# First gate and value products of a chunked-attention SwiGLU kernel, made in halves of 256 tokens

## The chip, the core and the metric

The kernel runs on one core of a Trainium2 chip. The metric is the time of one execution on the device in microseconds (us); lower is better. TensorE (PE in the rows) multiplies, VectorE (DVE), ScalarE (ACT) and GpSimd (POOL) work on tiles, SyncE (SP) issues most of the DMA transfers. Each engine runs its instructions in the order of its own queue; between the engines semaphores say when a tile is ready.

## What is computed

```python
# attention in chunks of 64 tokens: B=8, H=8, S=576, D=64
scores = (1 / sqrt(D)) * q_c @ k_c.T            # one chunk with itself
attn = exp(scores - max); attn = attn / (sum(attn) + 1e-9)
out = attn @ v_c                                # -> x: 4608 tokens x 512
# gated layer: d_model 512, d_ff 1536
rms = sqrt(mean(x * x) + 1e-6); xn = x / rms * rms_g
g = xn @ w_gate; silu = g / (1 + exp(-g))
y = (silu * (xn @ w_val)) @ w_out               # 4608 x 512
```

## The kernel before

The 4608 tokens go in tiles of 512 (`TT`), each of two units of 256 (`UT`). The first three tiles are worked in plain form, the others in pairs. Every product of the gated layer is made three times, as high part by high part, high by low and low by high (`up`, L591; `down`, L626): a single precision number is split in two parts that TensorE multiplies fully. d_ff is cut into 12 blocks `f` of 128. For one `f` of a plain tile, `up` makes 12 products 128x512 into the bank `ps_g` (4 slices of d_model, 3 products each) and 12 into `ps_v`; `gated` then makes the silu on ScalarE (L609, with a load of its function table where another function ran before), multiplies it with `ps_v` on VectorE (L613), and splits the result into `gh` (L614, ScalarE) and `gl` (L618, VectorE); `down` of the `f` before follows on TensorE.

Both banks come from `ps_h`, a pool of two banks. The `ps_g` of the next `f` therefore lies in the bank that the silu of this `f` reads, and its first product waits for that silu. The two other pools are `ps_a` (two banks) and `ps_acc` (four, for the sums of `down` from the first `f` on).

Ahead of the first products stands a prologue. Units 0 and 1 (four half units 0 to 3) go through scores (`scores`, L265), softmax (`softmax` L278 to L282 for unit 0, `softmax_both` L570 to L576 for unit 1), a transpose of the exponentials (`att_transpose` L323 on TensorE, copied by L324 on ScalarE), the row sums (`softmax_sum` L287 to L289), the value products (`att_values` L450), the scaling by the sums (`first_norm` L536), the squares (`first_squares` L548 on ScalarE), the root of their mean (`first_root`, L144 on ScalarE and L145 on GpSimd) and the scaling by it (`first_scale` L556 and L560, ScalarE). Then the tokens of a unit are turned: `x_turn_unit` transposes them on TensorE (L510, four blocks 128x128 to a bank), `x_high_unit` makes the high part `xh` (L516, ScalarE) and `x_low_unit` the low part `xl` (L522, VectorE).

Beside this the weights are converted from 64-bit raw words, block after block: `conv_load` (L169, a DMA of SyncE), `conv_start` (L177 and L178, each 128x1024, ScalarE), `conv_join` (L186, L187, L190 on VectorE, L203 on ScalarE for the high part, L205 as a DMA of SyncE that puts a copy `wfd` into DRAM), `conv_end` (L211, VectorE, the low part). `conv_step` loads block n+4, starts n+1, joins n and ends n-1. In the program text the prologue ends with `conv_start(0)` and `conv_step(EARLY)`, that is three steps; later steps stand inside `gated`. In the first tile, at `f` = 0, `load_unit` (L233 to L235) issues the transfers `qt`, `kt`, `vt` of unit 2, and its scores follow on TensorE.

In this part of the program a scheduler sets each engine's order: it takes what is ready by its estimate, by a priority that follows the place in the program text. `urgent()` raises the priority of the silu and what follows it by `URGENT` = 300. Only from the second tile on is TensorE's order written by hand.

Of the kernel before, what the change touches and what calls it, by code (L numbers as in the profile page):

```python
# [13 lines left out]
AF = mybir.ActivationFunctionType  # L14
# [9 lines left out]
UT = 256  # L24
NU = N // UT
TT = 512
# [3 lines left out]
NDT = DM // P  # L30
DFF = 1536
NF = DFF // P
SCALE = D**-0.5
# [46 lines left out]
def tile_chunk_attn_swiglu(  # L80
# [124 lines left out]
                nc.sync.dma_start(wfd[f], w)  # L205

    def conv_end(n):
        if 0 <= n < len(pairs):
            w, parts = conv.pop(n)
            hi, lo = (parts[:, i].rearrange("p i c -> p (i c)") for i in range(2))  # L210
            nc.vector.tensor_tensor(lo, w, hi.bitcast(F32), op=ALU.subtract)  # L211
# [350 lines left out]
    def softmax_both(u, banks):  # L562
        both = [state[2 * u + s] for s in range(2)]
        es = [att.tile([P, NPAIR, 2, CH], F32, name="e") for _ in both]
        mx = small.tile([P, 2, 2, NPAIR, 1], F32, name="mx_u")
        for st, e in zip(both, es):
            st["e"] = e
        for j in range(2):
            by_row = banks[j].rearrange("p s (a k) -> p s a k", k=CH)
            nc.vector.tensor_reduce(mx[:, j], by_row, axis=AX.X, op=ALU.max)  # L570
            for s, (st, e) in enumerate(zip(both, es)):
                nc.vector.tensor_tensor(
                    e[:, :, j], st["s"][j], mx[:, j, s].broadcast_to([P, NPAIR, CH]), op=ALU.subtract
                )
        for e in es:
            nc.scalar.activation(e, e, AF.Exp, scale=SCALE)  # L576

    def softmax_whole(u, banks):
        softmax_both(u, banks)
# [3 lines left out]
        nc.vector.tensor_scalar_add(rs, rs, 1e-9)  # L583
        nc.vector.reciprocal(rs, rs)

    def up(wh, wl, f, name):
        ps = bank(ps_h, name)
        for dt in range(NDT):
            cols = slice(dt * P, (dt + 1) * P)
            for i, (a, b) in enumerate(((wh, xh), (wh, xl), (wl, xh))):  # L590
                nc.tensor.matmul(  # L591
                    ps,
                    a[f][:, cols],
                    b[dt],
                    start=(dt == 0 and i == 0),
                    stop=(dt == NDT - 1 and i == 2),
                )
        return ps

    def gated(f, at, then):  # L600
        pg = up(wgh, wgl, f, "ps_g")
        pv = up(wvh, wvl, f, "ps_v")
        if 0 in at:
            then()
        sg = tmp_tile("sg")
        gh = gp.tile([P, TT], F32R, name="gh")
        gl = gp.tile([P, TT], F32R, name="gl")
        with urgent():
            nc.scalar.activation(sg, pg, AF.Silu)  # L609
        if 1 in at:  # L610
            then()
        with urgent():
            nc.vector.tensor_tensor(sg, pv, sg, op=ALU.mult)  # L613
            nc.scalar.copy(gh, sg)  # L614
        if 2 in at:
            then()
        with urgent():
            nc.vector.tensor_tensor(gl, sg, gh.bitcast(F32), op=ALU.subtract)  # L618
        return gh, gl
# [505 lines left out]
    first_squares(0)  # L1125
    first_root(0)
    first_scale(0, False)
    att_transpose(2)
    softmax_sum(2)
    att_transpose(3)  # L1130
    softmax_sum(3)
    o = two_banks(ps_h, "ps_o")
    att_values(2, o)
    first_norm(2)
    o = two_banks(ps_acc, "ps_o")
# [3 lines left out]
    first_root(1)  # L1139
    first_scale(1, False)  # L1140
    for d in range(0, NDT, 2):
        x_turn_unit(0, d, ps_a)
        x_high_unit(0, d)
        x_low_unit(0, d)
    for d in range(0, NDT, 2):
        x_turn_unit(1, d, ps_a)
        x_high_unit(1, d)
        x_low_unit(1, d)
    conv_start(0)
    conv_step(EARLY)  # L1150

    for t in range(PLAIN):
        if t == 1:
# [36 lines left out]
        acc = [ps_acc.tile([P, DM], F32, tag="acc", name=f"acc{s}") for s in range(NSUB)]  # L1190
        prev = None
        for f in range(NF):
            g = gated(f, CONVS[f % 2], conv_step)
            if t == 0:
                if f in (0, 5):
                    u = 2 + (f == 5)
                    load_unit(u)
                    sc = two_banks(ps_a, "ps_s")
                    for i in (2 * u, 2 * u + 1):
                        scores(i, sc)  # L1200
                    if f:
                        softmax_rows(u, sc)
                    else:
                        softmax_whole(u, sc)
                elif f in (2, 7):
                    for i in (2 * u, 2 * u + 1):
                        att_transpose(i)
                elif f in (3, 8):
                    o = two_banks(ps_a, "ps_o")
                    for i in (2 * u, 2 * u + 1):  # L1210
                        att_values(i, o)
                    norm_unit(u, o)
                if f == NF - 1:
                    x_transpose((0, 1))
            elif t == 1 and f == NF - 1:
                for dt in range(NDT):
                    x_split(dt, blocks(x)[:, :, dt], slice(0, TT))
            if t == 1:
                if f % 2 == 0:
                    save_plain(f // 2)  # L1220
                for todo in made.pop(0):
                    todo()
            if t:
                half()
            if prev is not None:
                down(acc, f - 1, *prev)
            if t:
                half()
            prev = g
# [89 lines left out]
```

## Time and profile before

| | us |
|---|---|
| runs | 901.83, 903.35, 903.49 (median 903.35) |
| the profiled execution | 903.58 |
| its span in the trace | 901.8 |
| TensorE busy in the span | 879.7 (98%) |
| VectorE, ScalarE, GpSimd busy | 604.8, 456.2, 183.9 |

The profiled execution lasts 1.8 us longer than its span; this lies around the first and the last instruction. The first 40 us, with the prologue, are the only longer part of the span in which TensorE is not busy throughout. The place to read is therefore one moment: when the second `ps_g`, that of `f` = 1, begins, and what set it.

### The profile page before, as it was taken

The numbers are of one execution on the slowest core, as the hardware profiler recorded it, in microseconds if no ns is written. First come the engines' busy times: TensorE is split into PE (matmuls) and PEld (weight loads), VectorE is DVE, ScalarE is ACT, GpSimd is POOL, SyncE is SP. The second block draws the span as 40 slices with busy tenths as digits, with TensorE's granted clock in tenths as the row PEclk, the third lists the DMA queues.
The fourth block names the chain that finished last, engine by engine and source line by source line (L and its number), as shares of the span: only waits on it lengthen the run. The fifth ranks groups of instructions, "written<-read, shape, count | busy, mean of one in ns | idle before, by whom it ended". The sixth has DMA issues, their size and how long they took to land.

```text
span 901.8 us, 17425 instructions
## 1 busy us (share of the span) xinstructions
PE 879.7 (98%) x6828; PEld 722.8 (80%) x6828; DVE 604.8 (67%) x962; ACT 456.2 (51%) x775; POOL 183.9 (20%) x157
## 2 busy tenths in 40 slices
PE   4899999999999999999999999999999999999998
PEld 3688888888888888888878888888888888888886
DVE  6999865464568755885577997555769953334775
ACT  5998934343445564544545644336447522222452
POOL 0004040243200000233323002333330004323200
PEclk9799999999999999999999999999999999999999
DMA  9699999777977864887797877685866794445442
GB/s 353 258 346 330 334 331 352 244 253 236 302 250 237 259 207 155 308 275 261 260 324 281 306 282 262 247 295 189 310 233 244 287 360 164 155 156 201 180 164 94
DMA packets 85794, 231.84 MB, mean 257 GB/s; under 512 B 8912, under 2 KB 45264, under 8 KB 71504
## 3 DMA queue, kind: packets, MB, share of 16 engines
q1 hardware_dynamic: 84656, 230.20, 72.4%
q8 instruction: 54, 0.88, 0.4%
q10 hardware_dynamic: 1056, 0.52, 0.2%
q14 instruction: 28, 0.23, 0.1%
HBM read 167.25 MB, written 63.44 MB: 256 GB/s over the span
## 4 chain that ended last, share of the span: by engine, by line
PE 90%; DMA 4%; DVE 2%; ACT 1%; POOL 1%; issue 1%; SPq 0%; POOLq 0%; ACTq 0%; DVEq 0%
PE ps_g L591 11%; PE acc L626 11%; PE ps_v L591 11%; PE ps_c L819 10%; PE ps_b L819 10%; PE ps_a L819 9%; PE ps_b L1032 5%; PE ps_c L1032 5%; PE ps_a L1032 5%; PE ps_d L819 5%; DMA wr<-wsd 3%; PE ps_d L1032 3%; PE ps_o L392 2%; PE ps_s L265 2%; DMA x<-qT_dram 1%
## 5 line engine op out<-in xcount | busy, mean ns | idle before, releaser
L819 PE MATMUL ps_c<-xp,wr 128*128 128x512 f32 x432 | 104.6, 391 | 0.5 <-DMA wr<-wsd 0.5
L819 PE MATMUL ps_b<-xp,wr 128*128 128x512 f32 x432 | 104.4, 391 | 0.0
L819 PE MATMUL ps_a<-xp,wr 128*128 128x512 f32 x432 | 103.6, 390 | 0.0
L591 PE MATMUL ps_g<-xh,parts 128*128 128x512 f32 x288 | 97.0, 397 | 0.6 <-ACT xh L516 0.6
L591 PE MATMUL ps_v<-xh,parts 128*128 128x512 f32 x288 | 95.2, 391 | 0.0
L819 PEld LDWEIGHTS ps_c<-xp,wr 128*128 128x128 f32 x432 | 80.6, 188 | 17.6 <-issue 0.7
L819 PEld LDWEIGHTS ps_a<-xp,wr 128*128 128x128 f32 x432 | 80.9, 188 | 16.9
L819 PEld LDWEIGHTS ps_b<-xp,wr 128*128 128x128 f32 x432 | 80.7, 188 | 17.0
L626 PE MATMUL acc<-parts,gh 128*128 128x512 f32 x288 | 89.9, 393 | 0.0
L907 POOL TENSOR_TENSOR g<-u,u 128x512 f32<-128x512 f32 x18 | 23.2, 1290 | 268.3 <-ACT u L875 130.3
L591 PEld LDWEIGHTS ps_g<-xh,parts 128*128 128x128 f32 x288 | 54.7, 190 | 12.7 <-ACT xh L516 1.0
L591 PEld LDWEIGHTS ps_v<-xh,parts 128*128 128x128 f32 x288 | 54.5, 189 | 11.3
L939 ACT CAST gh<-g 128x512 fp32r<-128x512 f32 x72 | 43.5, 621 | 37.3 <-PE ps_b L1032 13.3
L626 PEld LDWEIGHTS acc<-parts,gh 128*128 128x128 f32 x288 | 53.2, 188 | 11.2
L944 DVE TENSOR_TENSOR gl<-g,gh 128x512 fp32r<-128x512 f32 x72 | 50.3, 705 | 15.8 <-PE ps_a L1032 7.0
L897 POOL TENSOR_TENSOR p<-p,p 128x512 f32<-128x512 f32 x36 | 46.8, 1311 | 52.9 <-DVE rs L353 35.8
L591 PE MATMUL ps_g<-xl,parts 128*128 128x512 f32 x144 | 56.7, 394 | 0.0
L591 PE MATMUL ps_v<-xl,parts 128*128 128x512 f32 x144 | 56.3, 391 | 0.0
L626 PE MATMUL acc<-parts,gl 128*128 128x512 f32 x144 | 56.2, 390 | 0.0
L875 ACT ACTIVATE p<-p 128x512 f32<-128x512 f32 x36 | 22.8, 633 | 58.4 <-POOL p L897 52.6
L819 PE MATMUL ps_d<-xp,wr 128*128 128x512 f32 x216 | 52.3, 391 | 0.0
L884 DVE TENSOR_TENSOR u<-ps_b,p 128x512 f32<-128x512 f32 x36 | 24.5, 687 | 40.0 <-PE ps_b L819 36.4
(150 smaller groups left out, 1705.2 us busy)
## 6 DMA issues: line engine op xcount, KB each, us to landing
wr<-wsd SPq DMA_DIRECT2D x63, 1024.0 KB, 7.1
wo<-osd SPq DMA_DIRECT2D x30, 1024.0 KB, 7.7
raw<-w_up_dram SPq DMA_DIRECT2D x12, 1024.0 KB, 9.9
vt<-v_dram SPq DMA_DIRECT2D x18, 512.0 KB, 6.0
wsd<-parts SPq DMA_DIRECT2D x18, 512.0 KB, 8.2
qt<-qT_dram SPq DMA_DIRECT2D x17, 512.0 KB, 5.2
kt<-kT_dram SPq DMA_DIRECT2D x17, 512.0 KB, 6.1
away_e<-e SPq DMA_DIRECT2D x28, 256.0 KB, 3.3
```

The source lines that it names most:

```text
L265: nc.tensor.matmul(st["s"][j][c * CH : (c + 1) * CH, pr], st["q"][rows, pr, tok : tok + CH], st["k"][rows, pr, tok : tok + CH], start=True ...
L392: nc.tensor.matmul(st["o"][(2 * c + t) * Q : (2 * c + t + 1) * Q, h * D : (h + 1) * D], eT[c][rows, t, h], vt[rows, c, h], start=True, sto ...
L591: nc.tensor.matmul(ps, a[f][:, cols], b[dt], start=(dt == 0 and i == 0), stop=(dt == NDT - 1 and i == 2),)
L626: nc.tensor.matmul(acc[s], a[:, cols], b, start=(f == 0 and i == 0), stop=(f == NF - 1 and i == 2),)
L819: nc.tensor.matmul(ps, w[:, a, m, cols], xp[:, b, kt], start=start and kt == 0 and i == 0, stop=stop and kt == 1 and i == 2, skip_group_ch ...
L875: nc.scalar.activation(t, t if src is None else src, AF.Silu)
L884: nc.vector.tensor_tensor(kp["u2"], b["b"], kp["p1"], op=add)
L897: nc.gpsimd.tensor_tensor(kp["p5"], kp["p1"], kp["p5"], op=add)
L907: nc.gpsimd.tensor_tensor(g[:, 0, 1], kp["u2"], kept[0]["u2"], op=mult)
L939: nc.scalar.copy(gh, src)
L944: nc.vector.tensor_tensor(gl, src, pair[0].bitcast(F32), op=ALU.subtract)
L1032: nc.tensor.matmul(banks[m][name], w[:, (0, 1, 0)[k], m * P : (m + 1) * P], (gh, gh, gl)[k], start=opens and i == 0 and k == 0, stop=not ( ...
```

## The change

The first block, `f` = 0 of the first tile, is made in two halves of 256 tokens. `up` gets its bank and a slice of tokens; `gated` gets `begun`, the two banks that already hold the first half's products, and makes the second half's into them. Where 24 products 128x512 stood, there are now 48 of 128x256. Unit 0 is turned and split right behind the row sums of unit 1 in the program text, in banks of `ps_acc`, and block 0 of the weights is started and joined before the transposes of unit 1 and ended behind the split of unit 0. The exps of `softmax_both` get a priority raised by 600. `ps_o` of half unit 2 comes from `ps_acc` instead of `ps_h`, since `begun` now holds `ps_h`. Behind `begun` stand `conv_load(4)`, `conv_start(1)` and two conversion steps from block 1 on, in place of the three from block 0.

```diff
--- before.py
+++ after.py
@@ -205,7 +205,7 @@
                 nc.sync.dma_start(wfd[f], w)
 
     def conv_end(n):
-        if 0 <= n < len(pairs):
+        if n in conv:
             w, parts = conv.pop(n)
             hi, lo = (parts[:, i].rearrange("p i c -> p (i c)") for i in range(2))
             nc.vector.tensor_tensor(lo, w, hi.bitcast(F32), op=ALU.subtract)
@@ -572,8 +572,9 @@
                 nc.vector.tensor_tensor(
                     e[:, :, j], st["s"][j], mx[:, j, s].broadcast_to([P, NPAIR, CH]), op=ALU.subtract
                 )
-        for e in es:
-            nc.scalar.activation(e, e, AF.Exp, scale=SCALE)
+        with tc.high_priority(offset=2 * URGENT):
+            for e in es:
+                nc.scalar.activation(e, e, AF.Exp, scale=SCALE)
 
     def softmax_whole(u, banks):
         softmax_both(u, banks)
@@ -583,23 +584,27 @@
         nc.vector.tensor_scalar_add(rs, rs, 1e-9)
         nc.vector.reciprocal(rs, rs)
 
-    def up(wh, wl, f, name):
-        ps = bank(ps_h, name)
+    def up(wh, wl, f, ps, tokens=slice(0, TT)):
         for dt in range(NDT):
             cols = slice(dt * P, (dt + 1) * P)
             for i, (a, b) in enumerate(((wh, xh), (wh, xl), (wl, xh))):
                 nc.tensor.matmul(
-                    ps,
+                    ps[:, tokens],
                     a[f][:, cols],
-                    b[dt],
+                    b[dt][:, tokens],
                     start=(dt == 0 and i == 0),
                     stop=(dt == NDT - 1 and i == 2),
                 )
         return ps
 
-    def gated(f, at, then):
-        pg = up(wgh, wgl, f, "ps_g")
-        pv = up(wvh, wvl, f, "ps_v")
+    def gated(f, at, then, begun=None):
+        if begun is None:
+            pg = up(wgh, wgl, f, bank(ps_h, "ps_g"))
+            pv = up(wvh, wvl, f, bank(ps_h, "ps_v"))
+        else:
+            pg, pv = begun
+            up(wgh, wgl, f, pg, slice(UT, TT))
+            up(wvh, wvl, f, pv, slice(UT, TT))
         if 0 in at:
             then()
         sg = tmp_tile("sg")
@@ -1125,11 +1130,18 @@
     first_squares(0)
     first_root(0)
     first_scale(0, False)
+    conv_start(0)
+    conv_join(0)
     att_transpose(2)
     softmax_sum(2)
     att_transpose(3)
     softmax_sum(3)
-    o = two_banks(ps_h, "ps_o")
+    for d in range(0, NDT, 2):
+        x_turn_unit(0, d, ps_acc)
+        x_high_unit(0, d)
+        x_low_unit(0, d)
+    conv_end(0)
+    o = two_banks(ps_acc, "ps_o")
     att_values(2, o)
     first_norm(2)
     o = two_banks(ps_acc, "ps_o")
@@ -1139,15 +1151,18 @@
     first_root(1)
     first_scale(1, False)
     for d in range(0, NDT, 2):
-        x_turn_unit(0, d, ps_a)
-        x_high_unit(0, d)
-        x_low_unit(0, d)
-    for d in range(0, NDT, 2):
         x_turn_unit(1, d, ps_a)
         x_high_unit(1, d)
         x_low_unit(1, d)
-    conv_start(0)
-    conv_step(EARLY)
+    first = slice(0, UT)
+    begun = [
+        up(wgh, wgl, 0, bank(ps_h, "ps_g"), first),
+        up(wvh, wvl, 0, bank(ps_h, "ps_v"), first),
+    ]
+    conv_load(AHEAD)
+    conv_start(1)
+    conv_at[0] = 1
+    conv_step(EARLY - 1)
 
     for t in range(PLAIN):
         if t == 1:
@@ -1190,7 +1205,8 @@
         acc = [ps_acc.tile([P, DM], F32, tag="acc", name=f"acc{s}") for s in range(NSUB)]
         prev = None
         for f in range(NF):
-            g = gated(f, CONVS[f % 2], conv_step)
+            g = gated(f, CONVS[f % 2], conv_step, begun)
+            begun = None
             if t == 0:
                 if f in (0, 5):
                     u = 2 + (f == 5)
```

From the second tile on the order of all engines is that of before, and GpSimd's is the same throughout. Line numbers of the functions behind the exps are larger by 1 (L577), 5 (L614 for the silu L609, L619 for L614, L618 for L613, L623 for L618, L631 for L626).

On ScalarE, from the cast of one weight block to the first silu, before (`xh_119` to `xh_122` are the four slices of d_model; `raw` is a block of weights):

```order
L516 ACTIVATE xh_122<-ps_x,g_col 128x256
L516 ACTIVATE xh_119<-ps_x,g_col 128x256
L516 ACTIVATE xh_120<-ps_x,g_col 128x256
L203 CAST parts<-w 128x1024
L177 ACTIVATE w<-raw 128x1024
L516 ACTIVATE xh_121<-ps_x,g_col 128x256
L516 ACTIVATE xh_122<-ps_x,g_col 128x256
L178 ACTIVATE raw<-raw 128x1024
L203 CAST parts<-w 128x1024
L177 ACTIVATE w<-raw 128x1024
L609 ACT_TABLE_LOAD
L609 ACTIVATE sg<-ps_g 128x512
```

and after:

```order
L178 ACTIVATE raw<-raw 128x1024
L556 ACTIVATE x<-x,ri_u 128x512
L560 ACTIVATE x<-x,ri_u 128x512
L203 CAST parts<-w 128x1024
L516 ACTIVATE xh_119<-ps_x,g_col 128x256
L516 ACTIVATE xh_120<-ps_x,g_col 128x256
L516 ACTIVATE xh_121<-ps_x,g_col 128x256
L516 ACTIVATE xh_122<-ps_x,g_col 128x256
L203 CAST parts<-w 128x1024
L178 ACTIVATE raw<-raw 128x1024 x2
L614 ACT_TABLE_LOAD
L614 ACTIVATE sg<-ps_g 128x512
```

Behind the scaling of unit 1 (L560) all four `xh` of unit 1 now stand in a row; two L178 stand between the casts and the silu, where an L178, a cast and an L177 stood. Counted from the scaling of unit 0, there are now five L178 and three L177 ahead of the silu, where there were three and four; all else on the way there has the same count.

On TensorE, from the last value products of the prologue to the first gate products, before:

```order
L450 MATMUL ps_o_397<-vt,eT 64x64 x2
L450 MATMUL ps_o_396<-vt,eT 64x64 x2
L450 MATMUL ps_o_397<-vt,eT 64x64 x2
L510 MATMUL ps_x<-ident,x 128x128 x12
L591 MATMUL ps_g<-xh_119,parts 128x512
L591 MATMUL ps_v<-xh_119,parts 128x512
L510 MATMUL ps_x<-ident,x 128x128 x4
L591 MATMUL ps_g<-xl_123,parts 128x512
L591 MATMUL ps_g<-xh_119,parts 128x512
L591 MATMUL ps_g<-xh_120,parts 128x512
```

and after, at the transposes of unit 1 (the first half's 24 products lie ahead of them, the second half's behind; `xl_123` is the low part's first slice):

```order
L591 MATMUL ps_v<-xh_121,parts 128x256
L591 MATMUL ps_v<-xh_122,parts 128x256
L591 MATMUL ps_v<-xl_126,parts 128x256
L591 MATMUL ps_v<-xh_122,parts 128x256
L510 MATMUL ps_x<-ident,x 128x128 x8
L591 MATMUL ps_g<-xh_119,parts 128x256
L591 MATMUL ps_v<-xh_119,parts 128x256
L591 MATMUL ps_g<-xl_123,parts 128x256
L591 MATMUL ps_g<-xh_119,parts 128x256
L591 MATMUL ps_g<-xh_120,parts 128x256
L591 MATMUL ps_v<-xl_123,parts 128x256
```

The transposes of unit 0, eight of the twelve in one row before, now stand behind the scores of half unit 3, and products of 256 columns stand on both sides of those of unit 1.

On SyncE, around the transfers of unit 2 (`qt`, `kt`, `vt`), before:

```order
L205 DMA wfd_128<-w 128x1024
L169 DMA raw<-w_out_dram 128x1024
L205 DMA wfd_129<-w 128x1024
L169 DMA raw<-w_up_dram 128x1024 x2
L233 DMA qt<-qT_dram 128x1024
L205 DMA wfd_130<-w 128x1024
L234 DMA kt<-kT_dram 128x1024
L235 DMA vt<-v_dram 128x1024
```

and after:

```order
L205 DMA wfd_128<-w 128x1024
L169 DMA raw<-w_up_dram 128x1024
L169 DMA raw<-w_out_dram 128x1024
L205 DMA wfd_129<-w 128x1024
L169 DMA raw<-w_up_dram 128x1024 x2
L205 DMA wfd_130<-w 128x1024
L233 DMA qt<-qT_dram 128x1024
L234 DMA kt<-kT_dram 128x1024
L235 DMA vt<-v_dram 128x1024
```

Before, `qt` stood ahead of the third copy of weights, `wfd_130`, and `kt` and `vt` behind it; now all three stand behind it.

## Rows read from the trace of the kernel before

**Rows 1.** The page: span, busy time, and the granted clock in 40 slices

```profile
span 901.8 us, 17425 instructions
...
PE 879.7 (98%) x6828; PEld 722.8 (80%) x6828; DVE 604.8 (67%) x962; ACT 456.2 (51%) x775; POOL 183.9 (20%) x157
...
PEclk9799999999999999999999999999999999999999
```

**Rows 2.** Waits of TensorE, 31 to 360 us: us in total, times, longest

```profile
PE ps_g L591 <- ACT xh L516: 0.6, 1, 0.6
```

**Rows 3.** Timeline of TensorE, 27 to 42 us: start, us, [idle before it]

```profile
29.63 0.33 PE L510 MATMUL ps_x<-ident,x 128*128 128x128 f32 x1 [2.48 <-ACT x L556]
30.24 0.90 PE L510 MATMUL ps_x<-ident,x 128*128 128x128 f32 x3 [0.28 <-ACT x L560]
...
40.18 0.39 PE L591 MATMUL ps_g<-xh,parts 128*128 128x512 f32 x1
```

**Rows 4.** ScalarE in one stretch: us, busy us (instructions), granted clock, DMA, GB/s

```profile
17.98:39.24 21.26, 20.36 (x32) 0.68 0.81 334
```

**Rows 5.** ScalarE by line in that stretch: count, busy us, mean ns, idle

```profile
L177 ACT ACTIVATE w<-raw 128x1024 f32<-128x1024 f32 x4 | 4.6, 1149 | 0.0
L178 ACT ACTIVATE raw<-raw 128x1024 int32<-128x1024 uint32 x3 | 3.5, 1155 | 0.0
```

**Rows 6.** Timeline of ScalarE, 26 to 43 us

```profile
28.86 0.72 ACT L556 ACTIVATE x<-x,ri_u 128x512 f32<-128x512 f32 x1 [0.45 <-POOL ri_u L145]
29.48 0.71 ACT L560 ACTIVATE x<-x,ri_u 128x512 f32<-128x512 f32 x1
...
31.18 0.84 ACT L516 ACTIVATE xh<-ps_x,g_col 128x256 fp32r<-128x256 f32 x2 [0.27 <-PE ps_x L510]
...
34.62 1.19 ACT L178 ACTIVATE raw<-raw 128x1024 int32<-128x1024 uint32 x1
35.67 1.06 ACT L203 CAST parts<-w 128x1024 fp32r<-128x1024 f32 x1
...
37.80 1.28 ACT L609 ACT_TABLE_LOAD   x1
39.24 0.60 ACT L609 ACTIVATE sg<-ps_g 128x512 f32<-128x512 f32 x1 [0.16 <-PE ps_g L591]
```

**Rows 7.** Chain that ended last, 0 to 60 us: start, us, what

```profile
17.98 0.72 ACT x L556
...
40.34 2.72 PE ps_g L591 x12
...
48.50 1.09 PE ps_s L265 x64
...
55.72 0.87 PE ps_t L323 x8
```

**Rows 8.** Busy time and granted clock (PEclk) by stretches

```profile
20.00:26.60 6.60, 5.27 (x77) 4.57 (x78) 6.21 (x14) 6.60 (x10) 0.00 (x0) 0.50 1.02 421
26.70:30.00 3.30, 0.78 (x5) 0.35 (x3) 2.97 (x5) 2.85 (x9) 0.70 (x1) 1.00 1.00 415
30.10:36.80 6.70, 5.99 (x17) 4.62 (x18) 5.78 (x11) 6.43 (x12) 0.00 (x0) 0.50 0.73 300
36.90:44.00 7.10, 7.10 (x32) 5.82 (x32) 6.38 (x8) 6.92 (x9) 0.00 (x0) 1.00 0.13 52
```

**Rows 9.** Timeline of SyncE's queue, 15 to 60 us

```profile
42.30 0.33 SPq L205 DMA_DIRECT2D wfd<-w  x1
42.72 0.38 SPq L234 DMA_DIRECT2D kt<-kT_dram  x1
```

**Rows 10.** DMA issues in three short stretches: count, KB, us to landing

```profile
qt<-qT_dram SPq DMA_DIRECT2D x1, 512.0 KB, 10.2
...
kt<-kT_dram SPq DMA_DIRECT2D x1, 512.0 KB, 4.6
...
vt<-v_dram SPq DMA_DIRECT2D x1, 512.0 KB, 5.5
```

## The prediction

> **What bounds the kernel now.** First the page: TensorE is busy 879.7 of 901.8 us [rows 1], so the other engines matter only where they make it wait. Next its waits: between 31 and 360 us, and the three plain tiles lie in there, it waits once, 0.6 us for an `xh` [rows 2]. What lies behind the products of `f` = 0 is therefore one row of TensorE work, and whatever moves the start of `f` = 1 moves the end by as much. That start is 40.18 us [rows 3].
>
> Who sets it? TensorE itself: its products of `f` = 0 run up to 40.18 without a hole. But ScalarE is close behind. The bank of the second `ps_g` is the one that the silu reads; the silu starts at 39.24 and takes 0.60 [rows 6], so the bank is free at 39.84, 0.34 us before it is wanted. Whoever takes work off TensorE here gains at most 0.34 us, unless the silu comes earlier too. So ScalarE has to be read up to the silu. Both orders of ScalarE agree up to the first scaling of unit 0, at 17.98 [rows 7]. From there to the silu are 21.26 us, of which ScalarE is busy 20.36 [rows 4]; the 0.88 us that it stands idle are three waits: 0.45 for the root, 0.27 for the transposes, 0.16 for the last `ps_g` [rows 6]. ScalarE is thus full as well, and TensorE is not: it stood still 2.48 us ahead of 29.63, waiting for ScalarE's scaling of unit 1 [rows 3]. The prologue's bound is ScalarE, and the change moves no work off it.
>
> **The change part by part.** *ScalarE to the silu.* In the order of after the same instructions stand between the scaling of unit 0 and the silu, but for one thing: five L178 for three, three L177 for four. That is one more instruction of 128x1024. One takes 1.155 us in the mean [rows 5], but neighbours overlap a little: from the start of an L178 at 34.62 to that of the next at 35.67 are 1.05 us [rows 6]. This is +1.05. Its waits change too. The transposes of unit 0 are now wanted right behind the scaling of unit 0; behind the scaling of unit 1 the `xh` came 0.99 us later (29.48 and 0.71 make 30.19; 31.18 [rows 6]), and three transposes took 0.90 of that [rows 3]. So about 1.0 us idle, and 0.1 for the second copy of exponentials, for which no row speaks and which I bound by 0 and 0.45, the longest of the three waits. Against that the 0.45 for the root goes, since an L178 of 1.05 now stands between the squares' last step and the scaling; the 0.27 goes, since a cast stands ahead of the `xh` of unit 1; the 0.16 goes if TensorE is earlier. Idle is then 1.1 for 0.88, +0.2. The silu starts at 39.24 + 1.05 + 0.2 = 40.5 and ends at 41.1.
>
> *TensorE to `f` = 1.* The price of a product 128x256 is in no row. A row of twelve products 128x512 takes 2.72 us, 0.227 each [rows 7]; the half is 0.113 at best and 0.227 at worst. The nearest row is that of eight transposes 128x128 in 0.87, 0.109 each [rows 7], which is a floor under a tile that is half as wide; I take 0.113. The second half can begin when unit 1 is scaled. Counted back from the silu's start at 40.5, behind L560 come two casts and two L178 (four times some 1.05), four `xh` (0.84 for two, so 1.7) and the table load (1.28), 7.2 in all: the scaling of unit 1 ends near 33.3, where it was 30.19. It is three us later, because more of the weights' conversion stands ahead of it. Eight transposes and four `xh` on, near 35.7, TensorE needs for the 24 products 2.7 us at 0.113 and 5.4 at twice that. It is done between 38.4 and 41.1, not later than the silu's end. Whichever price holds, `f` = 1 begins when the silu has ended, at 41.15, and that is **+1.0 us**.
>
> [...]
>
> *The exps with raised priority, the banks.* They do nothing by themselves: the exps are the same two instructions, and their new place is in the order counted above. `ps_o` of half unit 2 in `ps_acc` finds these banks empty before `f` = 0 sums into them. Cost 0, and covered by ScalarE in any case.
>
> *SyncE.* `qt`, `kt`, `vt` of unit 2 now stand behind the third copy `wfd_130`; before, `qt` stood ahead of it, `kt` and `vt` behind. `kt` was issued at 42.72, behind the copy at 42.30 [rows 9], and landed 4.6 us later [rows 10], at 47.3; its scores began at 48.50 [rows 7]. If the copy stays at 42.30, `qt` goes at 42.7 and `kt` at 43.1, and with 4.6 to 5.5 [rows 10] it lands at 47.7 to 48.6. The scores are wanted at 48.50 + 1.0, less 0.7 because three of the twelve products of `down` now stand behind them: 48.8. Cost 0, with 0.2 to 1.1 us to spare; gone if the queue is full, as when `qt` took 10.2 [rows 10]. That is a rival below.
>
> *The other side of the swap.* The L177 that no longer stands ahead of the silu, and the casts behind, come later, but TensorE's only wait up to 360 us was the one of [rows 2], so I take 0 for the conversions and allow 0.4 for one that grazes.
>
> Sum: +1.0 on the profiled execution, from 903.58 (span 901.8) to 904.6 (span 902.8). The profiled execution stands 0.23 above the median 903.35, so by the median **904.4**.
>
> **The rivals.** *The clock is low when `f` = 1 begins.* [...] It fell behind the idle 2.48 us that end at 29.63 [rows 3], and rose again while the products of `f` = 0 ran. In after a like hole stands between the first half's products and 33.3, and if TensorE finishes the second half at 38.4, a second one of 2.7 us stands right ahead of `f` = 1. Then the stretch at half speed lies behind the start of `f` = 1, where it costs. Were it as long as that of before, 6.7 us, half of that would be lost, 3.3; if it has begun earlier and only its rest lies behind, 0.3 or 1. I take +1.6 on top: 904.4 + 1.6 = 906.0, slower. For it speaks the size of the hole; against it that the first hole lowers the clock first, and then the second half is itself slow, fills TensorE up to 41, and raises the clock as the first `f` did before. It decides if the granted clock still reads 0.50, or reads it again, when `f` = 1 begins.
> [...]
>
> *`kt` or `qt` lands late.* With 10.2 us for `kt` from an issue at 40 (the copy may go up to 2.7 us earlier, as its conversion starts earlier) it lands at 50.2, and the scores wait 50.2 - 48.8 = 1.4: 904.4 + 1.3 = 905.7. For it: three transfers and a copy in one row where `qt` was long there. Against: the queue moved 52 GB/s from 36.9 to 44.0, against 415 ahead of 30 [rows 8].
>
> *The change does what it aims at.* The silu isn't what is waited for, and `f` = 1 begins when the second half is done, at 38.5: 38.5 - 40.18 = -1.7, so 901.7. For this ScalarE would have to reach the silu 2.6 us earlier than summed, at 37.9. For it: `xh` of unit 0 and its products are out of the way early, and TensorE's 2.48 us are used. Against: the order counted above, where ScalarE has one instruction more and no idle time to give back.
>
> **How the numbers follow.** Forecast 904.4, chance 0.58; low clock, 906.0, 0.20; late transfer, 905.7, 0.08; gain, 901.7, 0.14. A measurement of this kernel can tell about 0.2% from no change, 1.8 us: faster means under 901.5, slower over 905.2. The runs of before alone lie 1.7 apart, so each case spreads: the forecast gives 0.01 faster, 0.49 same, 0.08 slower; the low clock 0.05 same and 0.15 slower; the late transfer 0.03 and 0.05; the gain 0.07 faster and 0.07 same. Together 0.08, 0.64, 0.28. The range leaves out about half of the gain below and the longest stretch of low clock above: 902.2 to 906.4.
>
> **What the profile would show.** Right: TensorE's first 128x512 product starts near 41.1, behind a wait for the silu; the silu starts near 40.5 with ScalarE busy throughout ahead of it; the scaling of unit 1 ends near 33.3; TensorE busy for the same 880 us, give or take 1. The low clock would show as a granted clock of 0.50 behind 41 us; the late transfer as a wait of the scores for `kt` near 48 us; the gain as a start of `f` = 1 ahead of 39 us. The forecast is wrong if products of 256 columns cost more than those of 512, or if TensorE's waits behind 60 us, now none, have grown.

## The result, and the profile after

The median after is 908.22 us (7 runs, 905.50 to 911.23), before 903.35 (7 runs, 901.51 to 904.68): the ratio is 1.0061, with a 95% interval of 1.0044 to 1.0077. The change costs 4.9 us, where 1.0 was forecast, and lies above the forecast's range. The profiled execution of after took 906.65.

The page of after, to be read against [rows 1]: the span, TensorE's busy time with its instructions, and a queue that brings instructions (fetches, MB, share); that it is TensorE's is worked out below.

```profile
span 904.9 us, 17477 instructions
PE 882.1 (97%) x6852; PEld 725.2 (80%) x6852; DVE 605.5 (67%) x962; ACT 457.7 (51%) x775; POOL 188.7 (21%) x157
q8 instruction: 54, 0.88, 0.4%
```

The span is 3.1 longer and TensorE busy for 2.4 more. What it now waits for, from 15 us to the end (in total, times, longest), against the one wait of [rows 2] up to 360 us; from 40 us to the end before waits for transfers alone, as the second rows show:

```profile
PE acc L631 <- issue: 1.0, 1, 1.0
PE ps_s L265 <- issue: 0.6, 1, 0.6
PE ps_g L591 <- ACT sg L614: 0.5, 1, 0.5
...
PE ps_c L824 <- issue: 0.3, 1, 0.3
```

```profile
PE ps_o L392 <- DMA eT<-away_e: 0.7, 2, 0.4
PE ps_c L819 <- DMA wr<-wsd: 0.5, 1, 0.5
```

Two things are new. One is the wait for the silu (L614) that was forecast. The others are three waits for "issue": the profile shows nothing of another engine or a transfer of data that ends them. They stand in the middle of rows of products whose operands had long been there, at 319, 578 and 612 us, far behind the prologue. First the forecast one, in TensorE's timeline (start, duration, instruction, idle time ahead), which answers to [rows 3]:

```profile
33.54 2.15 PE L510 MATMUL ps_x<-ident,x 128*128 128x128 f32 x8 [3.67 <-ACT x L556]
35.62 0.58 PE L591 MATMUL ps_g<-xh,parts 128*128 128x256 f32 x1
...
40.91 0.28 PE L591 MATMUL ps_v<-xh,parts 128*128 128x256 f32 x1
41.72 0.50 PE L591 MATMUL ps_g<-xh,parts 128*128 128x512 f32 x1 [0.53 <-ACT sg L614]
```

`f` = 1 starts at 41.72, 1.54 later than the 40.18 of [rows 3]; 0.97 was summed. The second half's products fill the time from 35.62 to 41.19, about up to the silu's start at 41.07. ScalarE's rows of that stretch, to be read against [rows 6], and its busy time from the scaling of unit 0 to the silu, against [rows 4]:

```profile
17.21 0.72 ACT L556 ACTIVATE x<-x,ri_u 128x512 f32<-128x512 f32 x1 [0.89 <-POOL ri_u L145]
...
19.54 0.84 ACT L516 ACTIVATE xh<-ps_x,g_col 128x256 fp32r<-128x256 f32 x2 [0.99 <-PE ps_x L510]
...
30.89 1.28 ACT L178 ACTIVATE raw<-raw 128x1024 int32<-128x1024 uint32 x1
32.76 0.72 ACT L556 ACTIVATE x<-x,ri_u 128x512 f32<-128x512 f32 x1 [0.59 <-POOL ri_u L145]
33.39 0.71 ACT L560 ACTIVATE x<-x,ri_u 128x512 f32<-128x512 f32 x1
...
41.07 0.60 ACT L614 ACTIVATE sg<-ps_g 128x512 f32<-128x512 f32 x1
```

```profile
17.21:41.07 23.86, 21.90 (x34) 0.86 0.74 298
```

The stretch is 23.86 us, where it was 21.26: 1.54 more busy, 1.06 more idle. That is 2.60, and 1.25 was summed. It shows as only 1.54 at `f` = 1 because unit 0's scaling began 0.77 earlier in this execution (17.21 against 17.98; it lies between 17.2 and 18.0 in all the traces of this study, in unmoved prologues too) and because the silu had 0.34 to spare before.

To see where all the rest arises, take the same product in both traces and subtract its start in before from that in the other kernel, each counted from the start of its span. This is the lag, in us, at moments of before's time:

| kernel | 41 | 290 | 310 | 335 | 440 | 475 | 600 | 626 | 890 |
|---|---|---|---|---|---|---|---|---|---|
| after | 1.7 | 1.7 | 2.0 | 2.9 | 2.9 | 2.7 | 3.3 | 4.2 | 3.1 |
| after, again (e1) | 1.9 | 2.9 | 3.8 | 5.6 | 5.6 | 4.0 | 4.5 | 7.7 | 6.7 |
| halves alone (e2) | -0.3 | -0.2 | -0.2 | 3.5 | 3.5 | 1.9 | 3.2 | 4.3 | 3.3 |
| before, 48 entries more (e5) | -0.6 | 1.4 | 2.4 | 3.5 | 3.6 | 2.0 | 3.0 | 4.1 | 3.1 |
| after, aligned (e12) | 2.2 | 3.1 | 3.2 | 3.7 | 3.7 | 3.3 | 5.8 | 5.8 | 5.7 |

The lag of after has a step at `f` = 1 and further steps near 301, 318, 576 and 610 us. The last three are the "issue" waits; at the first no wait shows in the rows, but a product starts 0.44 behind the one before it (301.84 and 301.40) where 0.23 is usual. Between 440 and 475, and near 631, it goes down: there before waited 0.5 for a transfer of weights and twice, 0.7 in all, for `eT`, and who comes late finds part of that done. The ends of the rows are the differences of the spans to within 0.2. So the one profiled execution of after is accounted for: 1.7 from `f` = 1, 2.7 at the four steps (1.9 of it in the three waits), less 1.2.

### The profile page after: what moved, and what is told of

The parts are those of the page before. It is cut to its first block, busy times and chain, and to the rows that moved or that the text cites. A ratio compares the mean times of both kernels' runs of the same rounds, so it can differ in the third digit from the quotient of the medians.

```text
span 904.9 us, 17477 instructions
## 1 busy us (share of the span) xinstructions
PE 882.1 (97%) x6852; PEld 725.2 (80%) x6852; DVE 605.5 (67%) x962; ACT 457.7 (51%) x775; POOL 188.7 (21%) x157
## 4 chain that ended last, share of the span: by engine, by line
PE 93%; DMA 2%; ACT 2%; DVE 1%; issue 1%; POOL 0%; SPq 0%; POOLq 0%; ACTq 0%
PE acc L631 11%; PE ps_g L591 11%; PE ps_c L824 11%; PE ps_v L591 11%; PE ps_b L824 10%; PE ps_a L824 10%; PE ps_b L1037 5%; PE ps_c L1037 5%; PE ps_a L1037 5%; PE ps_d L824 5%; PE ps_d L1037 3%; PE ps_o L392 2%; PE ps_s L265 2%; DMA wr<-wsd 2%; DMA x<-qT_dram 1%
## 5 line engine op out<-in xcount | busy, mean ns | idle before, releaser
L591 PE MATMUL ps_g<-xh,parts 128*128 128x512 f32 (+1 forms) x296 | 97.9, 392 | 0.6 <-ACT sg L614 0.5
L591 PE MATMUL ps_v<-xh,parts 128*128 128x512 f32 (+1 forms) x296 | 96.2, 386 | 0.0
L631 PE MATMUL acc<-parts,gh 128*128 128x512 f32 x288 | 90.1, 394 | 0.0
L631 PEld LDWEIGHTS acc<-parts,gh 128*128 128x128 f32 x288 | 53.1, 188 | 12.3 <-issue 1.2
L591 PE MATMUL ps_g<-xl,parts 128*128 128x512 f32 (+1 forms) x148 | 57.6, 389 | 0.1
L591 PE MATMUL ps_v<-xl,parts 128*128 128x512 f32 (+1 forms) x148 | 57.3, 387 | 0.0
L631 PE MATMUL acc<-parts,gl 128*128 128x512 f32 x144 | 56.1, 390 | 1.0 <-issue 1.0
```

Source lines behind the costliest of these rows:

```text
L591: nc.tensor.matmul(ps[:, tokens], a[f][:, cols], b[dt][:, tokens], start=(dt == 0 and i == 0), stop=(dt == NDT - 1 and i == 2),)
L631: nc.tensor.matmul(acc[s], a[:, cols], b, start=(f == 0 and i == 0), stop=(f == NF - 1 and i == 2),)
```

## The experiments

All ratios are to runs of the kernel before on the same chip, with a 95% interval. "`f` = 1" is the start of its first product in the profiled execution, from the start of the span (before 40.18, after 41.72).

**The same kernel again (e1).** No edit.

> The changed kernel unchanged, for a second trace and more times with their granted clocks. Three theories. S: ScalarE reaches the first silu later, and f=1 starts 1.5 to 2.5 us later than before. C: in some executions the clock is at its lower level behind the start of f=1, which costs 3 to 5 us in those. I: the 24 more products shift TensorE's program, and waits of the kind issue (1.9 us in all in the first trace) appear behind 300 us. S alone: all executions within 1 us of each other, near 905. C: times fall into two groups some 4 us apart, the long ones with a mean granted clock of 0.990 or 0.991, the short ones with 0.996. I: waits of the kind issue stand at the same products again, 1 to 2 us in all.

910.23 us, ratio 1.0079 (1.0057 to 1.0101); `f` = 1 at 41.92. The waits of TensorE in its profiled execution, whose span is 908.4:

```profile
PE acc L631 <- issue: 2.2, 1, 2.2
PE ps_t L323 <- ACT e L577: 1.8, 1, 1.8
PE ps_s L265 <- issue: 1.5, 1, 1.5
PE ps_g L591 <- issue: 0.5, 1, 0.5
PE ps_c L824 <- issue: 0.3, 1, 0.3
```

The same instructions wait, at the same places, for 4.5 us where they waited 1.9. `f` = 1 differs by 0.2 between the two executions, the "issue" waits by 2.6, most of the difference of the spans, 3.5. Behind the wait at 614 the granted clock was also low (0.64 from 614.4 to 617.0), where in after it was 1.00 (from 612.4 to 620.0).

**The halves alone (e2).** The kernel before with its first `f` in halves, and nothing moved.

```diff
+    first = slice(0, UT)
+    begun = [
+        up(wgh, wgl, 0, bank(ps_h, "ps_g"), first),
+        up(wvh, wvl, 0, bank(ps_h, "ps_v"), first),
+    ]
     for t in range(PLAIN):
...
-            g = gated(f, CONVS[f % 2], conv_step)
+            g = gated(f, CONVS[f % 2], conv_step, begun)
+            begun = None
```

> The kernel before, with the products of f=0 in halves but nothing moved: unit 0 is turned where it was, the conversion steps are where they were, so ScalarE's order is that of before. S: f=1 starts at 40.2 to 40.6 as before, time within 1 us of before (903 to 904.5). C: no hole ahead of f=1, mean clock 0.992 throughout as before, no long executions. I: waits of the kind issue behind 300 us appear as in the changed kernel, since as many products are more; time 904.5 to 905.5. If halves cost TensorE more than the whole (over 0.12 each at full clock), f=1 starts later than 40.6.

907.09 us, ratio 1.0059 (1.0039 to 1.0079), though `f` = 1 starts *earlier* than before, at 39.75. TensorE has 24 products more and finishes its two halves in time; it then waits 2.6 us for the silu. The loss lies elsewhere:

```profile
PE acc L630 <- issue: 2.6, 1, 2.6
PE ps_g L590 <- ACT sg L613: 2.6, 1, 2.6
PE ps_c L823 <- issue: 1.1, 1, 1.1
PE ps_s L265 <- issue: 0.9, 1, 0.9
```

These are after's three places, and no others. The longest shows the shape of all. The chain (start, duration, work) of before around 316 us, and then that of e2:

```profile
313.94 1.41 PE ps_o L392 x91
315.35 2.95 PE acc L626 x12
```

```profile
313.71 1.41 PE ps_o L392 x91
315.13 1.12 PE acc L630 x4
316.25 2.64 issue
318.89 3.44 PE acc L630 x8
```

The same twelve products are interrupted behind the fourth. The remaining eight take 3.44 us, 0.43 each, because the granted clock has fallen behind the wait (window; busy us and count; granted clock):

```profile
310.00:318.50 8.50, 6.25 (x149) 1.00 0.95 310
318.50:321.90 3.40, 3.01 (x8) 0.52 0.07 24
```

So one wait of 2.64 costs 3.7 (the lag goes from -0.2 to 3.5). It isn't so behind every wait of that length: behind e1's wait of 2.15 the clock stayed at 1.00 (322.6 to 326.0).

**The moves alone (e3).** After without the halves.

```diff
-    begun = [
-        up(wgh, wgl, 0, bank(ps_h, "ps_g"), first),
-        up(wvh, wvl, 0, bank(ps_h, "ps_v"), first),
-    ]
+    begun = None
```

> The changed kernel without the halves: unit 0 is turned early and all is moved as in the change, but the 24 products of f=0 have 512 columns and follow the turn of unit 1; ScalarE's order up to the silu is that of the changed kernel. S: the silu is held by TensorE here, whose 24 products begin near 35.5; at the lower clock (0.43 each) they end near 45, so f=1 starts 3 us later than in the changed kernel, time 908 to 910 with all executions alike. C: no hole ahead of f=1, since TensorE itself is what is waited for, so the times do not split. I: no waits of the kind issue, as the number of products is that of before.

906.59 us, ratio 1.0028 (1.0003 to 1.0052); `f` = 1 at 41.48. The `f` = 0 products run from 34.98 to 41.48 at a granted clock of 1.00, so `f` = 1 came earlier than expected. None of e1's four waits is there; against the expectation a single one of 0.9 stands at another place, at 483.57.

**ScalarE's order by hand (e4).** After, with unit 0's turn, the weight casts and the scaling of unit 1 put in an order meant to bring the silu early (the core of the edit).

```diff
+    by_hand = tc.manual_schedule(engines={mybir.EngineType.Activation})
...
     first_root(1)
+    conv_join(1)
     first_scale(1, False)
+    conv_start(2)
```

> The changed kernel with ScalarE's order written by hand from the scaling of unit 0 to the first gh: the squares, the root and the scaling of unit 1 come ahead of the conversions of the third and later weight blocks, and four of the 128x1024 instructions that stood ahead of the silu stand behind it. All that is computed is the same. S: the scaling of unit 1 ends near 31 instead of 34.1, the silu starts at 36 to 38 instead of 41.1, f=1 at 37 to 39.5: 2 to 4 us faster than the changed kernel and 0 to 2.5 faster than before (901 to 903.5). C: the hole ahead of unit 1 shrinks from 3.7 us to under 2, so no long executions. I: waits of the kind issue remain, 903 to 905. If ScalarE is not what holds f=1, it stays near 905 to 908.

912.22 us, ratio 1.0103 (1.0074 to 1.0132); the expectation was missed. The cast L203 of block 1, put ahead of the scaling, waits 2.64 us for VectorE and holds the scaling back to 31.58. Unit 2's scores run ahead of `f` = 1, which starts at 42.81, and the clock is low (0.51) from 31.4 to 41.6:

```profile
30.63 1.04 ACT L203 CAST parts<-w 128x1024 fp32r<-128x1024 f32 x1 [2.64 <-DVE w L190]
31.58 0.72 ACT L556 ACTIVATE x<-x,ri_u 128x512 f32<-128x512 f32 x1
```

Four "issue" waits add 4.7 (0.9, 1.7, 0.9, 1.2), at e1's four places.

**What the waits are.** Each instruction on TensorE's queue can be counted in the trace: every product, its weight load, and the semaphore instructions and drains. In after these are 6852 + 6852 + 187 + 3 = 13,894. On queue q8 stand 54 fetches with 0.88 MB, 16 KB each; 13,894 / 256 is 54.3. This fits a queue that brings TensorE's instructions, 256 entries a fetch. Counted like this, the first instruction behind each wait stands at:

| kernel | start us, entry modulo 256 |
|---|---|
| after | 319.67: 193; 578.52: 193; 612.48: 194 |
| e1 | 303.56: 194; 322.63: 193; 579.72: 193; 614.47: 194 |
| e2 | 318.89: 193; 578.21: 193; 612.66: 194 |
| e3 | 483.57: 194 |

The four waits of e4 stand at 193 and 194 too. And the last fetch on q8 ended 1.2 to 1.6 us ahead of each. This reads as TensorE reaching the first entry of a new block and the block not being there. In before, where no such wait is, no block begins sooner than 2.05 us behind the end of its fetch, if fetches and blocks are paired in order as these waits pair them.

How long a wait is follows from when its fetch begins. The same boundary (entry 5569) in three executions, in us:

| kernel | TensorE stops | fetch begins | fetch ends | TensorE goes on | wait |
|---|---|---|---|---|---|
| after | 318.69 | 317.06 | 318.34 | 319.67 | 1.0 |
| e1 | 320.48 | 320.23 | 321.37 | 322.63 | 2.2 |
| e2 | 316.25 | 316.32 | 317.45 | 318.89 | 2.6 |

The fetch takes 1.1 to 1.3 in each, and TensorE goes on 1.3 to 1.4 behind its end; what differs is that the fetch begins 1.6 ahead of the stop in after, and 0.1 behind it in e2.

The waits stand only where the entries ahead of them ran fast: 128 value products 64x64 with their weight loads are 256 entries, as many as a block, in 1.48 us, against 24 entries in 2.72 for twelve products 128x512. (The chain's row of 313.94 names 91 of them.) In before's timeline:

```profile
313.87 1.48 PE L392 MATMUL ps_o<-vt,eT 64*32 64x64 f32 x128
```

In before's times the last 288 entries ahead of such a boundary take 5.27 us at the fastest, and none waits; moved on by 48, four boundaries come where they take 5.0, 4.8, 5.2 and 5.0, and these are the four places. (At e3's place the 288 take 7.1 and only the last 128 are fast, 0.9, so the count of 288, chosen to fit the four, is a rough divide and not a law.) The 24 additional products of the halves are 48 entries. Of the 54 crossings counted in after three show a wait, as in e2; in e1, e4 and e5 there are four. They cost 0.3 to 2.6 us each. The next runs test this reading; its rival is that the halves' own products or moved transfers disturb something behind them.

**Before with 48 entries more (e5), and with 16 (e6).** Twelve (or four) products 64x64 of the identity into a free bank, made in an idle moment of the prologue, nobody reads them; nothing else is changed. Each is two passes with a weight load each, four entries, so 48 (or 16) in all (e12's trace has 104 passes for its 52 products, and the page as many weight loads as passes, 6828 of each in before).

```diff
+    idle = bank(ps_acc, "idle")
+    for _ in range(12):
+        nc.tensor.matmul(idle[:D, :D], ident[:D, :D], ident[:D, :D], start=True, stop=True)
     conv_start(0)
```

> The kernel before with 12 products 64x64 more, of the identity with itself, whose result nothing reads, in TensorE's idle time near 28 us. They take about 0.4 us there and make 48 entries in TensorE's queue, a weight load and a product for each of two passes; 48 is what 24 more products with their weight loads make in the changed kernel. The orders of ScalarE, VectorE and SyncE are those of before. Theory I, in its sharper form: TensorE's program is fetched in blocks of 16 KB, 256 entries; every wait of the kind issue so far stood at entry 193 or 194 of 256, about 1.3 us behind the end of such a fetch, and only where the 288 entries ahead of the boundary ran in under 5.3 us. By that, a shift of 48 brings four boundaries into such places (a gate product near 300 us, a down product near 317, an L819 product near 576, scores near 609), waits of 2 to 4.7 us in all, time 905 to 907. Theory S (ScalarE alone): f=1 starts as before, time 902 to 903.5.

> The same with 4 such products, 16 entries. I: by the same reckoning no boundary but one near 227 us comes close, so no waits of the kind issue over 0.5 us, time 902 to 903.5 as before. If the products as such cost the time, a third of what 12 cost.

e5: 907.24 us, ratio 1.0044 (1.0029 to 1.0060), `f` = 1 at 39.54. Its waits (L626 and L819 are before's numbers for the same lines):

```profile
PE acc L626 <- issue: 1.1, 1, 1.1
PE ps_s L265 <- issue: 0.9, 1, 0.9
...
PE ps_g L591 <- issue: 0.8, 1, 0.8
PE ps_c L819 <- issue: 0.6, 1, 0.6
```

All four places of e1, at entries 193 and 194, with none of the change's code. e6: 902.18, ratio 0.9989 (0.9975 to 1.0004), no such wait, `f` = 1 at 39.36. So the number of entries is enough for these waits; neither the halves nor the moved transfers are needed.

**After moved on to the next like place (e7), and e4's order improved likewise (e8).** 52 of the same products bring the halves' 48 entries to 256, a whole block.

```diff
+    idle = bank(ps_acc, "idle")
+    for _ in range(52):
+        nc.tensor.matmul(idle[:D, :D], ident[:D, :D], ident[:D, :D], start=True, stop=True)
     conv_load(AHEAD)
```

> The changed kernel with 52 such products (208 entries, with the 48 of the halves 256) in TensorE's hole ahead of and behind the turn of unit 1; the orders of ScalarE, VectorE and SyncE are those of the changed kernel. I: the boundaries stand where they stood before, the four waits go, time 904 to 906, 2.5 to 5 us faster than the changed kernel on this chip; what is left over before is the later start of f=1, 1 to 2 us. S alone: no gain, 908 to 911, or somewhat slower.

> As e4_chain_first, but the cast of weight block 1 behind the scaling of unit 1 (in e4 it waited 2.6 us for VectorE ahead of it) and the start of block 2 behind the xh of unit 1, with the same 52 products. S: the scaling of unit 1 ends near 30.2 instead of 32.9, f=2 starts at 47 to 48.5 (before 49.5, the changed kernel 51.3). I: no waits of the kind issue. Both: 900 to 902.5, faster than before by 0.5 to 2.5 us. If the conversions that now come later are waited for (as in e4 near 60 and 90 us, 0.1 to 0.2), up to 1 us of it goes.

e7: 905.25 us, ratio 1.0031 (1.0014 to 1.0048): no "issue" wait is left, but some of the added products got in the way of the turn of unit 1 and `f` = 1 came at 43.38. e8: 904.07, ratio 1.0035 (1.0007 to 1.0062), slower than expected and widely spread (902.11 to 913.17): none left either in its profiled execution, the fastest of its twelve. Its added products stood behind the turn, on the path:

```profile
32.56 5.11 PE L1171 MATMUL idle<-ident 64*64 64x64 f32 x84
```

61 ns a pass, where 17 had been estimated from `scores` (64 in 1.1 us), so `f` = 1 came at 41.75 and the gain of the order could not show.

**A better order (e9), and the same aligned (e11).** As e4, but the scaling of unit 1 stands between the two halves of a weight start and the cast behind the split. e11 adds 52 products into eight blocks of columns of two banks and alternating quarters, ahead of unit 1's squares, where TensorE is idle.

```diff
-    first_scale(1, False)
+    conv_start(2, lambda: first_scale(1, False))
...
+    conv_join(1)
```

> The changed kernel with ScalarE's order by hand as in e8, better spread: block 2 is started in the waits for the root and for the turn of unit 1, and the cast of block 1 stands behind the xh of unit 1. No products are added, so the boundaries of TensorE's blocks stand about as in the changed kernel. Everything is computed. S: the scaling of unit 1 ends near 30.5, f=2 starts at 46.5 to 48 (before 49.5, changed kernel 51.3), which is worth 1.5 to 3 us against before. I: the four waits at entry 193 or 194 of 256 are there and take 2 to 4.7 us. Both: 902 to 905, no gain over before in spite of the earlier start.

> As e9_chain_first_2, with 52 products 64x64 of the identity, spread over the array's quarters as the scores are (17 ns for each of two passes there), in TensorE's hole ahead of the turn of unit 1: 208 entries, 256 with those of the halves. I: the waits of the kind issue at entry 193 or 194 go (4.1 us in e9's trace). S: f=2 starts at 46.5 to 48.5. Both: 900 to 903, faster than e9 by 3 to 5 us and than before by 0 to 2.5; e9's waits at 65 and 99 us for conversions and exps that come later (1.6 us) stay. If it is as slow as e9, the boundaries are not what costs.

e9: `f` = 1 at 37.48, 2.7 ahead of before, and yet 908.14 us, ratio 1.0064 (1.0048 to 1.0080), slower than expected, with waits of 2.1, 1.0 and 0.9 at three of the places. e11: `f` = 1 at 37.84, no such wait, 902.50, ratio 1.0003 (0.9987 to 1.0019). The chain at the first place, in e9 and then in e11:

```profile
313.61 1.41 PE ps_o L394 x91
315.03 1.36 PE acc L633 x5
316.39 2.11 issue
```

```profile
313.66 1.41 PE ps_o L394 x91
315.08 2.97 PE acc L633 x12
```

By the two ratios the alignment is worth 0.6%, some 5.5 us. e11 is no faster than before all the same: of its lag of -3.5 at 60 us only -0.4 is left at 120, behind waits for a weight block (L213, 0.5 at 66 us) and for exponentials (L307, 1.2 at 99); the other 1.4 of the loss stand in no row of waits. What the early start wins is thus in part taken back by the weights' conversion and the softmax of the next units; no run here tried to mend that.

**After aligned (e12).** After, with e11's 52 products in the same idle time.

```diff
+    idle = [bank(ps_acc, f"idle{j}") for j in range(2)]
+    for k in range(52):
+        rows = slice(k // 2 % 2 * D, (k // 2 % 2 + 1) * D)
+        c = k % 2
+        nc.tensor.matmul(
+            idle[k // 2 % 2][c * D : (c + 1) * D, k % 8 * D : (k % 8 + 1) * D],
+            ident[rows, rows],
+            ident[rows, rows],
+            start=True,
+            stop=True,
+        )
     first = slice(0, UT)
```

> The changed kernel with the same 52 products, in TensorE's hole ahead of the turn of unit 1 (in e7 a part of them stood behind it and put f=1 off to 43.2 us). The orders of ScalarE, VectorE and SyncE are those of the changed kernel. I: no waits of the kind issue over 0.3 us; f=1 starts at 41.7 as in the changed kernel; time 903.5 to 905, slower than before by what f=1 comes later, 1 to 2 us, and 3 to 5 us faster than the changed kernel. S alone: 907 to 910 as the changed kernel.

904.55 us, ratio 1.0030 (1.0010 to 1.0049); `f` = 1 at 41.53. The four waits are gone. In the profiled execution, the longest of the twelve with 909.26, one stands at e3's place. Like e3 it has 187 semaphore entries where before has 188, so its blocks lie one entry off those of before; e7 has the same count and shows no wait there:

```profile
483.98 0.16 PE ps_o L392 x10
484.14 2.22 issue
486.36 0.33 PE ps_o L392 x12
```

Its clock fell behind the wait for the silu, as a rival of the prediction had it for the change itself:

```profile
41.60:45.10 3.50, 3.50 (x9) 0.51 1.01 295
```

## Why the prediction was wrong

**The split of the loss.** The moves without the halves cost 0.28% (e3), after without the four waits 0.30% (e12): 2.5 and 2.7 us. The halves alone cost 0.59% (e2), and 48 entries without any change 0.44% (e5): 5.3 and 4.0. Their sum of 6.5 to 8.0 is nearer to the 7.1 of e1 (0.79%) than to the 4.9 of the first runs; the intervals of some 0.2% to either side leave room for both. In short: at most 2.5 to 2.7 us are the later `f` = 1 and what hangs on it (e3's trace has 0.9 of an "issue" wait in it), and the other half or more goes with the waits at the block boundaries, read here as instruction supply. The later `f` = 1 is also more than the 1.54 of the two traces: e5 and e6, whose prologue is before's but for a few idle products, begin it at 39.54 and 39.36, so before's 40.18 is a late one, and after's 41.72 lies 2.2 to 2.4 behind them.

**The step that failed** is the first one, "whatever moves the start of `f` = 1 moves the end by as much", and with it the pricing of TensorE's 24 additional products: "Whichever price holds, `f` = 1 begins when the silu has ended". It priced them as TensorE time in the prologue, and rightly found that nothing hangs on that; e2 shows it, with `f` = 1 no later than before. But e2's lag goes from -0.3 at `f` = 1 to 3.3 at the end, by waits of 2.6, 1.1 and 0.9 far behind it; and e8's profiled execution, without such waits, has `f` = 1 1.6 late and its end 1.5 early (span 900.3). It put them at nothing as entries on TensorE's queue, which the profile's page counts (x6828 products before, x6852 after) and whose queue of fetches it lists. Nothing of before shows a wait for a fetch, so the bound from the nearest rows would have been zero to an unknown. What could have been read from before's trace is where its fast runs of entries lie, and where the block boundaries. The prediction named "if TensorE's waits behind 60 us, now none, have grown" as what would make it wrong, and that is what happened. (None is right up to 360 us [rows 2]; behind, before waits 1.2 us in all for transfers.)

**ScalarE to the silu: right in kind, too small.** The silu binds `f` = 1, as forecast, and the profile has that wait. The idle time for the transposes was put at about 1.0 and is 0.99. Two terms of the sum were mis-sized. One is the root: "Against that the 0.45 for the root goes, since an L178 of 1.05 now stands" ahead of the scaling. That L178 does stand there, at 30.89, yet ScalarE waits 0.59 behind it. The root on GpSimd (L145) takes 1.50 us where it took 0.70 in before; in e1, e7 and e12 it takes 1.56 to 1.61. Its row in before, then in after, and VectorE's row beside the latter:

```profile
28.12 0.70 POOL L145 TENSOR_TENSOR ri_u<-ss_u,mhalf 128x2 f32<-128x2 f32 x1 [10.17 <-ACT ss_u L144]
```

```profile
31.22 1.50 POOL L145 TENSOR_TENSOR ri_u<-ss_u,mhalf 128x2 f32<-128x2 f32 x1 [14.04 <-ACT ss_u L144]
```

```profile
32.00 0.69 DVE L186 TENSOR_SCALAR w<-w 128x1024 f32<-128x1024 f32 x1
```

In after, e1, e3 (1.15) and e7 the root ends 0.03 to 0.04 behind an L186 of VectorE; whether the one holds up the other was not tested. The other term is ScalarE's busy time, 1.54 more where 1.05 was summed. With both, the scaling of unit 1 ended at 34.10, where 33.3 was forecast, and the silu began at 41.07, where 40.5 was.

**The price of a product 128x256.** Taken as 0.113 with 0.227 as the upper end. In after's second half one follows the other every 0.213 at a granted clock of 0.50 (36.88, 37.31 and 37.52 for `ps_g`, `ps_v` and `ps_g`), in e2 every 0.12 at 1.00. Two halves make 0.24 where a product 128x512 takes 0.227, so the halves cost 0.01 more for each product of 512 columns, 0.3 us in all.

**The rivals.** The low clock at `f` = 1 (the rival's 6.7 us are the later stretch at 0.50 in [rows 8]): in the profiled execution of after it was low from 33.8 to 40.6 (in e1's from 34.8 to 41.6), ahead of `f` = 1, as argued against the rival, and ScalarE's row at 41.07 shows no wait for TensorE, so it cost nothing. In that of e12 it was low behind it, 41.6 to 45.1, and the lag grew from 1.3 at the first product to 3.1, 1.8 where the rival had 1.6. Which it is varies between executions; how often in after, two profiles cannot say. The windows of after:

```profile
33.80:40.60 6.80, 6.61 (x29) 5.74 (x28) 5.80 (x9) 6.73 (x10) 0.00 (x0) 0.50 0.70 287
...
41.72:51.32 9.60, 9.60 (x100) 7.81 (x101) 9.13 (x12) 8.79 (x11) 0.00 (x0) 1.00 0.99 364
```

The late transfer: the scores of unit 2 began at 49.43 behind products without a wait, so it fell. (Its sum has 1.4 in one place and 1.3 in the next; the first is right.) The gain: `f` = 1 at 38.5 did not come. e9 has its scaling early and `f` = 1 at 37.48, and shows that ScalarE's order, not the amount of work, was what kept the change from it; e11 shows that even with `f` = 1 2.3 earlier than before the kernel does not end clearly sooner, against the 1.7 us that the rival had put on 38.5.

**What stays open.** What sets the moment at which a fetch begins, and so why the same boundary costs 1.0 in one execution and 2.6 in another: at entry 5569 it began 1.19, 2.56 and 2.65 us after TensorE had begun the entry 256 earlier (after, e1, e2). Which waits bring the clock down is open too, and how the 4.9 us of the medians divide in the executions that have no profile.

## What to carry to other kernels

In these traces an instruction added to TensorE's queue moved every later one against the blocks of 256 entries, read here as those in which instructions are fetched, so a change at 30 us cost time at 300 and 600: 48 idle entries in the prologue brought four waits there, 3.4 us in all (e5). When TensorE shows "issue" waits amid products whose operands are ready, count its entries up to them, and look when the last fetch of instructions ended: the same remainder modulo 256 (here 193 or 194) and the same short time (here 1.2 to 1.6 us) at each place speak for the fetch. Then put the same number of idle entries into the old kernel, and fill up to a whole block in the new one, before judging the change itself.

## What was unexpected

- The waits read as a block of 256 entries coming late cost 0.3 to 2.6 us, three times in after and e2, four in e1 and e5; 48 entries that compute nothing make the kernel 0.44% slower (e5), 16 make no difference (e6).
- Behind a wait of 2.64 us the granted clock fell to 0.52 for 3.4 us (e2), so the wait cost 3.7; behind one of 2.15 it stayed at 1.00 (e1).
- Products 64x64 of one bank's region follow each other every 61 ns in e8 (84 passes in 5.11 us).
- The root of 128x2 on GpSimd took 0.70 us in before and 1.50 in after, where it ended 0.03 behind an L186 of VectorE; what set the difference was not tested.
